# Block-sparse attention followed by a token and channel mixer: gates of pairs 1 to 5 by four column tiles, and a new order of late loads

## The chip, the cores and the metric

The kernel runs on one core of a Trainium2 chip. The metric is the time of one execution on the device in microseconds (us); less is better. The profile is that of one execution, and its times count from the start of its span.

## What is computed

The inputs are q, k and v of 4 batches, 8 heads, 768 positions and 64 channels, and four weight matrices. The part of the reference that matters here:

```
k_rep = k.reshape(B, H, n_blocks, block, D).mean(axis=3)        # 12 blocks of 64 keys
gate_scores = np.einsum('bhsd,bhnd->bhsn', q, k_rep)            # 768 queries x 12 blocks
gate_scores = np.where(causal, gate_scores, -1000000000.0)
top_idx = np.argsort(gate_scores, axis=-1)[..., -top_k:]        # top_k = 3, and the own block
...                                                             # a mask of the chosen blocks
scores = scale * np.matmul(q, k.transpose(0, 1, 3, 2))          # masked, causal, softmax
x = attention output, heads side by side (4, 768, 512)
h = np.maximum(xt @ w_tok1, 0.0) @ w_tok2                       # token mixing, 768 -> 256 -> 768
u = x + h.transpose(0, 2, 1)
h2 = np.maximum(u @ w_ch1, 0.0) @ w_ch2                         # channel mixing, 512 -> 1536 -> 512
return (u + h2).astype(np.float32)
```

The gate decides for each query which three blocks of keys it sees besides its own. It must be exact enough for the ranking, and so it is computed in 32-bit floats.

## The kernel before, in words

**Pairs.** Two heads of one batch make a pair; there are 16 pairs, four to a batch. Pair i goes through these steps, named as in the code (line numbers of the profile in brackets).

- Loads `kl` and `ql` (L315), two DMAs each on SyncE's queue, in the order kl.0, ql.0, kl.1, ql.1 and so on. A ring of three buffers holds each kind, so load i waits until the transposes of i-3 are done.
- Transposes `tr` of keys and queries on TensorE (L360), six 128x128 transposes each, and copies `kt` and `qt` out of PSUM by ScalarE (L369).
- Casts of kt and qt to 16 bits by GpSimd (L376), four of them for a pair. GpSimd also issues the loads of the values `v.i` (L322) and of the weights, which convert to 16 bits on the way. A load is put into GpSimd's program behind a cast that a table names: VAFTER for the values, WAIT for the weights.
- Block sums of the keys by VectorE (L389, L397), into `ks2`, 32 columns wide, of which 24 are used (two heads of 12 blocks).
- The gate. For pairs 0 to 5, `gate` (L407) holds 128 queries at a time as the stationary operand and streams the 24 columns of block sums: five such matmuls, for queries 128 to 767. Its result has queries on the partitions, which VectorE needs for the next step. Pairs 6 and 7, 8 to 11, and 12 to 15 go in groups: `gate_t` (L417) holds the block sums of each pair of the group in a 32-column tile of the array and streams the queries, so that the result is transposed; ScalarE copies it out (L427), and `gate_b` (L437) transposes it back.
- The ranking by VectorE (L449 or L453, L465, L473, L485), a transposition of the mask on TensorE (`mask`, L495), and two copies into rows 64 to 87 of the queries (L501), so that the scores matmul adds the mask by itself.
- For each head, scores in three parts (`sc`, L515), exponentials on ScalarE (L528), the causal corner on VectorE (L535), the product with the values (`av`, L547), and the division (L555, L566).

**Mixer.** When a batch has its four pairs, the token mixer (`tok1`, L578 or L609, and `umix`, L590 or L623) and the channel mixer follow: `ch1` (L659), 24 pieces of four matmuls, and `ch2` (L680), 18 pieces of four. They need the weights W0 and W1 (token), W2 to W5 (w_ch1 in quarters) and W6 to W9 (w_ch2 in quarters). Mixer work of one batch is put between the attention of the next.

**Order.** The program's order on every engine is written by `plan`, a list scheduler that runs when the program is built. Each step has an engine, a cost in ns, the steps it depends on, a priority, and buffers from rings. The costs and the sizes of transfers only decide the order; on the chip each engine runs its list in order and waits by semaphores. Where the planner sees TensorE free in the first 46 us it puts in small matmuls without use (`dummy`, L697), which keep the engine busy. PSUM holds two large tiles (`big`, for transposes, scores and the group gates) and three banks (`bank`, for the rest), so a transposition waits for a large tile whose copy by ScalarE is done.

The lines that decide the order of the loads:

```
O["v", i] = op("POOL", 1060, 0, last_av, vpre + 2, load_v(i), size=1350)
...
for i, (name, m) in enumerate(VAFTER):
    O["v", i].deps.append(O["cast", name, m, 1])
...
W.append(op("POOL", 700, 0, [O[("cast",) + WAIT[n]]], at, f, size=4500 if n < 2 else 2400 if n < 6 else 2800))
```

Of the kernel before, what the change touches and what calls it, by code (L numbers as in the profile page):

```python
# [9 lines left out]
FP = mybir.dt.float32  # L10
# [18 lines left out]
R = 5  # L29
# [10 lines left out]
def QACT(i):  # L40
    return i < 1


VAFTER = [("kt", 1), ("kt", 2), ("qt", 2), ("qt", 3), ("qt", 3), ("kt", 4), ("qt", 4), ("qt", 5),
          ("qt", 6), ("qt", 7), ("qt", 8), ("qt", 9), ("qt", 10), ("qt", 11), ("qt", 12), ("qt", 13)]
GATE = {2: 700, 3: 700, 4: 730}
GROUPED = [[0], [1], [2], [3], [4], [5], [6, 7], [8, 9, 10, 11], [12, 13, 14, 15]]
WAIT = [("kt", 3, 1), ("kt", 3, 1), ("qt", 3, 1), ("qt", 3, 1), ("qt", 4, 1), ("qt", 4, 1),
        ("qt", 5, 1), ("qt", 5, 1), ("qt", 6, 1), ("qt", 6, 1)]


class Op:
# [168 lines left out]
def kernel(  # L221
# [27 lines left out]

    pairs = [(b, h) for b in range(B) for h in range(0, H, 2)]  # L250
    NP = len(pairs)
    RINGS = dict(big=2, bank=3, av=1, ql=3, kl=3, qt=4, kt=2, gs=1, gt=1, gm=1, m8=1, bn=NBN, e0=3, e1=3, e2=3, rc=2,
                 x16=2, h1=2, u=2, uT=2, h2=1, ob=3)

    def sb(tag, shape, dt, name):
        return sp.tile(shape, dt, tag=tag, bufs=RINGS[tag], name=name)

# [25 lines left out]
    ident16 = sp.tile([128, 128], F16, tag="id16", name="id16")  # L283
    tri = sp.tile([128, 128], F16, tag="tri", name="tri")
    m0 = sp.tile([128, 128], F16, tag="m0", name="m0")
    warm = sp.tile([128, 256], F16, tag="warm", name="warm")
    spare = sp.tile([128, 8], F16, tag="spare", name="spare")

# [103 lines left out]
    def kcopy(i):  # L392
# [6 lines left out]
                                        axis=AX.X, op=ALU.add)  # L399
        return f  # L400

    def gate(i):
        def f():
            g = ps("bank", [128, GJ, 1, 2 * NB], "gps")
            T["gps", i] = g
            for j in range(GJ):
                nc.tensor.matmul(out=g[:, j, 0, :], lhsT=T["qt", i][:, 128 * j + 128:128 * j + 256],  # L407
                                 rhs=ks2[i % R][:, 0:2 * NB], start=True, stop=True)
        return f

    def gate_t(gi):
        def f():
            p = ps("big", None, "gtp")
            T["gtp", gi] = p
            for a, e in ((0, 512), (512, S - 128)):
                for s, i in enumerate(GROUPED[gi]):
                    nc.tensor.matmul(out=p[32 * s:32 * s + 32, a:e], lhsT=ks2[i % R],  # L417
                                     rhs=T["qt", i][:, 128 + a:128 + e], start=True, stop=True,
                                     tile_position=(0, 32 * s))
        return f  # L420

    def gate_e(gi):
        def f():
            n = 32 * len(GROUPED[gi])
            t = sb("gt", [128, S - 128], FP, f"gt_{gi}")
            T["gt", gi] = t
            nc.scalar.copy(out=t[0:n, :], in_=T["gtp", gi][0:n, 0:S - 128])  # L427
        return f

    def gate_b(gi):  # L430
        def f():
            n = 32 * len(GROUPED[gi])
            p = ps("big", None, "gbp")
            g = p[:, 0:128 * GJ].rearrange("p (j s c) -> p j s c", s=4, c=32)
            T["gps", GROUPED[gi][0]] = g[:, :, 0:len(GROUPED[gi]), 0:2 * NB]
            for j in range(GJ):
                nc.tensor.transpose(out=p[:, 128 * j:128 * j + n], in_=T["gt", gi][0:n, 128 * j:128 * j + 128],  # L437
                                    identity=ident32[0:n, 0:n])
        return f

# [275 lines left out]
    def prepare(i):  # L716
        b, h = pairs[i]
        gi = [n for n, G in enumerate(GROUPED) if i in G][0]
        i0 = GROUPED[gi][0]
        pre = 10.0 * (i0 - (AHEAD if i < FIRST else LATER)) + 2.5 * (i - i0) - (0 if len(GROUPED[gi]) == 1 else EXTRA)  # L720
        vpre = 10.0 * (i - (AHEAD if i < FIRST else LATER))
        old = i - R

        def last_scores(x):
            return [O.get(("sc", old, x, g)) for g in range(3)]

        for t32, src, off in (("kl", k, 0), ("ql", q, 0.1)):
            bf = Buf(t32)
            O[t32, i] = op("SP", 950, 0, [], pre - 12 + off, load_qk(i, t32, src), [bf], size=1750)
            big = Buf("big")  # L730
            O["tr", t32, i] = pe(660, [O[t32, i]], pre + off, transposes(t32, i), [big], tail=320)
            bf.users.append(O["tr", t32, i])
            name = "kt" if t32 == "kl" else "qt"
            tb = Buf(name)
            O[name, i] = act(768, [O["tr", t32, i]],
                             pre + 0.5 + off, evac_t(t32, i), [tb])
            big.users.append(O[name, i])
            dst = KA if name == "kt" else QA
            for x in range(2):
                occ = 770  # L740
                if QACT(i):
                    O["cast", name, i, x] = act(768, [O[name, i]] + last_scores(x), pre + 0.9 + 0.2 * x + off, cast_act(dst, name, i, x))
                    tb.users.append(O["cast", name, i, x])
                    continue
                O["cast", name, i, x] = op("POOL", occ, occ + 55, [O[name, i]] + last_scores(x), pre + 4 + off,
                                           cast(dst, name, i, x))
                tb.users.append(O["cast", name, i, x])
            if name == "kt":
                O["ksum", i] = dve(870, [O["kt", i]], pre + 1, ksum(i))
                tb.users.append(O["ksum", i])  # L750
                O["kcopy", i] = dve(200, [O["ksum", i], O.get(("gate", old))], pre + 1, kcopy(i))
            else:
                qb = tb
        last_av = [O.get(("av", i - R - 1, x)) for x in range(2)]
        O["v", i] = op("POOL", 1060, 0, last_av, vpre + 2, load_v(i), size=1350)
        n = len(GROUPED[gi])
        O["qb", i] = qb
        if i == GROUPED[gi][-1]:
            G = GROUPED[gi]
            if n == 1:  # L760
                gb = Buf("bank")
                O["gate", i] = gate_op = pe(1120, [O["kcopy", i], O["qt", i]], pre + 2, gate(i), [gb])
            else:
                tbig = Buf("big")
                gate_op = pe(GATE[n], [O["kcopy", m] for m in G] + [O["qt", m] for m in G], pre + 2, gate_t(gi), [tbig])
                for m in G:
                    O["gate", m] = gate_op
                gtb = Buf("gt")
                ge = act(S - 128, [gate_op], pre + 2.1, gate_e(gi), [gtb])
                tbig.users.append(ge)  # L770
                gb = Buf("big")
                gback = pe(550, [ge], pre + 2.2, gate_b(gi), [gb])
                gtb.users.append(gback)
            for m in G:
                O["qb", m].users.append(gate_op)
            gs = Buf("gs")
            O["gm", gi] = dve(75 + 125 * n, [gate_op] if n == 1 else [gback, own_op], pre + 3, gm(gi), [gs])
            gb.users.append(O["gm", gi])
            tops = [dve(720, [O["gm", gi]], pre + 3, top(gi, s)) if s == 0 else None for s in range(n)]
            for s in range(1, n):  # L780
                tops[s] = dve(720, [tops[0]], pre + 3, top(gi, s))
            O["lt", gi] = dve(75 + 125 * n, tops, pre + 3, below(gi))
            O["bias", gi] = dve((75 + 125 * n) if n == 4 else 200 * n, [O["lt", gi], O.get(("mask", gi - NBN))] + ([own_op] if n == 4 else []), pre + 3, bias(gi))
            gs.users += [O["bias", gi]]
            O["lt", gi].two = O["bias", gi].two = True
            mb = Buf("bank")
            O["mask", gi] = pe(280, [O["bias", gi]], pre + 4, mask(gi), [mb])
            for s, m in enumerate(G):
                for x in range(2):
                    O["put", m, x] = dve(410, [O["mask", gi]] + [O.get(("sc", m - R, x, g)) for g in range(3)],  # L790
                                         pre + 4, put_mask(gi, s, x))
                    mb.users.append(O["put", m, x])
# [45 lines left out]
        O["cast", "kt", 0, x].deps.append(O["qt", 0])  # L838
    O["ksum", 1].deps.append(O["bias", 0])
    for n, (at, f) in enumerate(wq):  # L840
        W.append(op("POOL", 700, 0, [O[("cast",) + WAIT[n]]], at, f, size=4500 if n < 2 else 2400 if n < 6 else 2800))

    for b in range(B):
        fill = 1000.0 * (b + 1)
# [78 lines left out]
    with tc.manual_schedule():  # L923
# [22 lines left out]
        nc.vector.memset(QAX[64:MK, :, :, 0:128], 0.0)  # L946
        for r in range(R + 1):
            nc.gpsimd.memset(V16[r][:, :, :, 64:65], 1.0)
        for y in range(NBN):
            nc.gpsimd.memset(bn16[y].bitcast(FP), 0.0)  # L950

# [35 lines left out]
```

## Time and profile before

| what | value |
|---|---|
| time, median of 5 runs | 264.81 us (263.87 to 266.32) |
| the profiled execution: its own time, its span | 264.81 us, 262.7 us |
| TensorE matmuls: busy, share of the span | 254.5 us, 97% |
| VectorE, ScalarE, GpSimd busy | 157.2, 145.3, 80.1 us |
| chain of work that ended last, TensorE's share | 92% |
| six direct gates (L407), matmuls | 60, start 8.4 to 48.8 us |
| three group gates (L417), matmuls | 40, start 60.6 to 136.1 us |
| V loads issued by GpSimd | 16, from 14.6 to 125.4 us |
| wc loads issued by GpSimd | 8, from 28.1 to 59.3 us |

A 32-bit matmul of the program is two instructions in the trace: five gate matmuls are ten. Matmuls overlap in the pipeline, so the cost of one is the distance from its start to the start of the next, not its duration. The view of waits says who waited for whom; the timeline of one engine shows in brackets how long it was idle before an instruction. A DMA lands when its last completion signal comes; these times are in the trace's DMA records.

### The profile page before, as it was taken

How to read it: one execution, taken by the hardware profiler on the slowest of the kernel's cores; microseconds unless marked ns; L12 is line 12 of the kernel's file. 1: busy time of each engine (PE TensorE's matmuls, PEld its weight loads, DVE VectorE, ACT ScalarE, POOL GpSimd, SP SyncE). 2: the span in 40 equal slices, each digit the busy share in tenths (PEclk: the TensorE clock that was granted, in tenths of full speed). 3: DMA queues.
4: the chain of work that ended last, by engine and by line, in shares of the span. 5: the costliest groups of instructions: out<-in, count | busy, mean ns of one | idle time of the engine just before them, and what ended most of it. 6: DMA issues, size and time to landing. Idle time of an engine off the chain costs nothing.

```text
span 262.7 us, 5828 instructions
## 1 busy us (share of the span) xinstructions
PE 254.5 (97%) x2296; PEld 165.9 (63%) x2296; DVE 157.2 (60%) x536; ACT 145.3 (55%) x195; POOL 80.1 (30%) x112
## 2 busy tenths in 40 slices
PE   8999999989899998999999999999999999999994
PEld 7988688875567685456656666654456544456443
DVE  3688769995967669985549965583243253333222
ACT  3877888857688964658863799940034400044000
POOL 8299638878236963245420000000000000000000
PEclk9999999999999999999999999999999999999999
DMA  8999999999999999187511000009220035300032
GB/s 167 221 187 192 204 189 190 189 190 190 184 135 214 191 209 125 40 115 117 72 41 44 0 2 0 2 0 202 80 80 2 0 63 137 130 32 0 2 146 93
DMA packets 91322, 28.77 MB, mean 110 GB/s; under 512 B 84896, under 2 KB 87840, under 8 KB 91296
## 3 DMA queue, kind: packets, MB, share of 16 engines
q1 hardware_dynamic: 63232, 21.33, 39.8%
q0 software_dynamic: 28064, 7.08, 27.2%
q8 instruction: 18, 0.29, 0.5%
q14 instruction: 8, 0.07, 0.1%
HBM read 26.83 MB, written 6.29 MB: 126 GB/s over the span
## 4 chain that ended last, share of the span: by engine, by line
PE 92%; DMA 3%; DVE 2%; ACT 1%; issue 1%; DVEq 0%; SPq 0%; ACTq 0%
PE c L659 24%; PE c L680 23%; PE sps L515 13%; PE avp L547 7%; PE tkl L360 4%; PE avp L697 3%; PE tql L360 3%; PE ups L590 3%; DMA kl<-in_k_dram 3%; PE gps L407 3%; PE tok L578 2%; PE gtp L417 1%; PE tok L609 1%; PE ups L623 1%; PE bps L495 1%
## 5 line engine op out<-in xcount | busy, mean ns | idle before, releaser
L528 ACT ACTIVATE e<-sps 128x1024 f16<-128x1024 f32 (+1 forms) x96 | 84.5, 920 | 15.8 <-PE sps L515 13.1
L659 PE MATMUL c<-uT,wc 128*128 128x256 f16 (+1 forms) x384 | 69.1, 326 | 0.0
L680 PE MATMUL c<-wc,h 128*128 128x512 f16 (+2 forms) x300 | 65.6, 370 | 0.0
L669 ACT ACTIVATE h<-c 128x512 f16<-128x512 f32 x48 | 28.7, 599 | 61.2 <-PE c L659 43.0
L659 PEld LDWEIGHTS <-wc 128*128 128x128 f16 x384 | 36.5, 98 | 23.0 <-issue 0.2
L515 PE MATMUL sps<-QA,KA 88*128 88x512 f16 (+3 forms) x256 | 50.2, 305 | 0.6 <-ACT e L528 0.6
L680 PEld LDWEIGHTS <-h 128*128 128x128 f16 x300 | 28.7, 98 | 30.5 <-issue 0.8
L376 POOL CAST KA<-kt 64x768 f16<-64x768 f32 x30 | 24.7, 824 | 44.3 <-ACT kt L369 27.0
L535 DVE TENSOR_TENSOR e<-e,m 128x256 f16<-128x256 f16 x90 | 28.1, 319 | 15.8 <-ACT e L528 15.1
L671 DVE TENSOR_SCALAR h<-c 128x256 f16<-128x256 f32 x48 | 20.3, 422 | 26.4 <-PE c L659 26.0
L688 DVE TENSOR_TENSOR ob<-u,c 128x512 f32<-128x512 f16 (+2 forms) x25 | 16.5, 664 | 32.2 <-PE c L680 32.1
L515 PEld LDWEIGHTS <-KA 88*128 88x128 f16 x256 | 22.9, 99 | 17.8 <-issue 1.2
L376 POOL CAST QA<-qt 64x768 f16<-64x768 f32 x30 | 25.7, 857 | 5.8 <-ACT qt L369 4.4
L547 PEld LDWEIGHTS <-e 128*128 128x128 f16 x672 | 25.3, 97 | 2.6
L547 PE MATMUL avp<-V,e 128*128 128x65 f16 x672 | 26.5, 193 | 0.0
L369 ACT COPY kt<-tkl 128x768 f32<-128x768 f32 x16 | 12.8, 799 | 11.7 <-PE tkl L360 8.4
L566 DVE TENSOR_TENSOR x<-avp,rc 128x384 f16<-128x384 f32 x32 | 17.8, 555 | 0.9
L389 DVE TENSOR_REDUCE kst<-kt 128x12 f32<-128x768 f32 x16 | 15.2, 950 | 5.0 <-ACT kt L369 4.6
L322 POOL DMA_DIRECT2D V<-in_v_dram x16 | 16.5, 1030 | 4.4 <-PE avp L547 3.2
L369 ACT COPY qt<-tql 128x768 f32<-128x768 f32 x16 | 12.8, 801 | 5.3 <-PE tql L360 5.1
L501 DVE COPY QA<-bps 24x640 f16<-24x640 f16 x32 | 14.3, 480 | 1.7 <-PE bps L495 1.4
L360 PE MATMUL tql<-id,ql 128*128 128x128 f32 x96 | 13.3, 275 | 1.9 <-ACT kt L369 1.0
(66 smaller groups left out, 212.8 us busy)
## 6 DMA issues: line engine op xcount, KB each, us to landing
kl<-in_k_dram SPq DMA_DIRECT2D x32, 192.0 KB, 5.8
ql<-in_q_dram SPq DMA_DIRECT2D x32, 192.0 KB, 5.9
out_dram<-ob SPq DMA_DIRECT2D x23, 256.0 KB, 2.0
V<-in_v_dram POOLq DMA_DIRECT2D x16, 192.0 KB, 7.1
wc<-in_moe_w_ch_dram POOLq DMA_DIRECT2D x8, 384.0 KB, 10.4
w<-in_moe_w_tok_dram POOLq DMA_DIRECT2D x2, 384.0 KB, 8.6
out_dram<-ob SPq DMA_DIRECT2D x1, 160.0 KB, 1.8
out_dram<-ob SPq DMA_DIRECT2D x1, 96.0 KB, 1.7
```

Source lines behind the costliest of these rows:

```text
L360: nc.tensor.transpose(out=p[:, 128 * j:128 * j + 128], in_=t[:, j, :], identity=ident32)
L369: nc.scalar.copy(out=t, in_=p[:, 0:S])
L376: nc.gpsimd.tensor_copy(out=to, in_=src)
L515: nc.tensor.matmul(out=p[:, off + a:off + a + n], lhsT=KA[i % R][x][0:MK, 128 * kk:128 * kk + 128], rhs=QA[i % R][x][0:MK, q0 + a:q0 + a + ...
L528: nc.scalar.activation(out=e[:, 0:width], in_=T["sps", i, x, g][:, 0:width], func=AF.Exp, scale=scale)
L535: nc.vector.tensor_tensor(out=d, in0=d, in1=m0.rearrange("p (a b) -> p a b", a=1).broadcast_to([128, 2, 128]), op=ALU.mult)
L547: nc.tensor.matmul(out=p[:, jq, :], lhsT=T["e", i, x, g][:, o:o + 128], rhs=V16[i % (R + 1)][:, x, kk, :], start=(kk == 0), stop=(kk == jq))
L566: nc.vector.tensor_tensor(out=T["x16", b][:, :, 64 * hh:64 * hh + 64], in0=T["aps", i, x][:, :, 0:64], in1=T["rc", i, x].broadcast_to([128 ...
L659: nc.tensor.matmul(out=p, lhsT=wc1_16[:, cc, 128 * fc:128 * fc + 128], rhs=T["uT", b][:, cc, a // 128:e // 128, :], start=(cc == 0), stop= ...
L669: nc.scalar.activation(out=T["h2", b][:, fc, a:e], in_=T["c1", b, fc, n], func=AF.Relu)
L671: nc.vector.tensor_scalar(out=T["h2", b][:, fc, a:e], in0=T["c1", b, fc, n], scalar1=0.0, scalar2=None, op0=ALU.max)
L680: nc.tensor.matmul(out=T["c2", b, j, lo], lhsT=T["h2", b][:, fc, 128 * j:128 * j + 128], rhs=wc2_16[:, fc, lo:hi], start=(fc == 0), stop=( ...
```

## The change

The gates of pairs 1 to 5 are computed as the groups are, but with one pair in all four column tiles: the same block sums are loaded into four 32-column tiles, and each tile streams another 128 of the pair's queries (queries 256 to 767). Four more matmuls of 64 columns cover queries 192 to 255 (all four tiles stream the same queries, so that all partitions of the result are written). Queries 128 to 191 can only choose among three blocks, all of which they see, and their gate values are set to zero once at the start. ScalarE copies 192 columns out (`gate_s`), and two transposes bring them back (`gate_r`): one of 32 partitions by 128 columns, one of 128 by 128. Pair 0 keeps the direct gate, now `gate_q`. The group gates leave out the same 64 queries: 576 columns in place of 640.

The tables VAFTER and WAIT name later casts: v.5 moves from behind the key cast of pair 4 to behind its query cast, v.6 to v.11 from behind the query casts of pairs 4, 5, 6, 7, 8, 9 to behind those of 6, 8, 11, 12, 13, 14, v.12 to the key cast and v.13 to v.15 to the query cast of pair 15. W6 and W7 move from the query cast of pair 5 to that of pair 6, W8 and W9 from that of 6 to that of 8. The planner's costs of gates and its sizes of V and of W6 to W9 change. The core of the diff:

```
-VAFTER = [("kt", 1), ("kt", 2), ("qt", 2), ("qt", 3), ("qt", 3), ("kt", 4), ("qt", 4), ("qt", 5),
-          ("qt", 6), ("qt", 7), ("qt", 8), ("qt", 9), ("qt", 10), ("qt", 11), ("qt", 12), ("qt", 13)]
-GATE = {2: 700, 3: 700, 4: 730}
+VAFTER = [("kt", 1), ("kt", 2), ("qt", 2), ("qt", 3), ("qt", 3), ("qt", 4), ("qt", 6), ("qt", 8),
+          ("qt", 11), ("qt", 12), ("qt", 13), ("qt", 14), ("kt", 15), ("qt", 15), ("qt", 15), ("qt", 15)]
+DIRECT = (0,)
+WSIZE = (2400, 4500)
+GATE = {1: 400, 2: 1000, 3: 1000, 4: 1000}
...
-        ("qt", 5, 1), ("qt", 5, 1), ("qt", 6, 1), ("qt", 6, 1)]
+        ("qt", 6, 1), ("qt", 6, 1), ("qt", 8, 1), ("qt", 8, 1)]
...
     def gate(i):
         def f():
-            g = ps("bank", [128, GJ, 1, 2 * NB], "gps")
-            T["gps", i] = g
-            for j in range(GJ):
-                nc.tensor.matmul(out=g[:, j, 0, :], lhsT=T["qt", i][:, 128 * j + 128:128 * j + 256],
-                                 rhs=ks2[i % R][:, 0:2 * NB], start=True, stop=True)
+            g = ps("bank", [128, 512], "gps")
+            T["gtp", i] = g
+            T["gps", i] = g[:, 192:192 + 32 * GJ].rearrange("p (j s c) -> p j s c", s=1, c=32)[:, :, :, 0:2 * NB]
+            for lo, at, n, step in ((256, 64, 128, 128), (192, 0, 64, 0)):
+                for s in range(4):
+                    nc.tensor.matmul(out=g[32 * s:32 * s + 32, at:at + n], lhsT=ks2[i % R],
+                                     rhs=T["qt", i][:, lo + step * s:lo + step * s + n], start=True, stop=True,
+                                     tile_position=(0, 32 * s))
+        return f
+
+    def gate_s(i):
+        return lambda: nc.scalar.copy(out=g1[i % 2][:, 64:256], in_=T["gtp", i][:, 0:192])
+
+    def gate_r(i):
+        def f():
+            g, t = T["gtp", i], g1[i % 2]
+            nc.tensor.transpose(out=g[:, 192:224], in_=t[0:32, 0:128], identity=ident32[0:32, 0:32])
+            nc.tensor.transpose(out=g[:, 224:352], in_=t[:, 128:256], identity=ident32)
         return f
...
-            for a, e in ((0, 512), (512, S - 128)):
+            for a, e in ((0, 512), (512, S - 192)):
...
-            nc.scalar.copy(out=t[0:n, :], in_=T["gtp", gi][0:n, 0:S - 128])
+            nc.scalar.copy(out=gt[0:n, 64:S - 128], in_=T["gtp", gi][0:n, 0:S - 192])
...
-        O["v", i] = op("POOL", 1060, 0, last_av, vpre + 2, load_v(i), size=1350)
+        O["v", i] = op("POOL", 1060, 0, last_av, vpre + 2, load_v(i), size=1800)
...
-                O["gate", i] = gate_op = pe(1120, [O["kcopy", i], O["qt", i]], pre + 2, gate(i), [gb])
+                split = i not in DIRECT
+                O["gate", i] = gback = gate_op = pe(GATE[1] if split else 1120, [O["kcopy", i], O["qt", i]], pre + 2, gate(i) if split else gate_q(i), [gb])
+                if split:
+                    tbuf = Buf("g1")
+                    gs1 = act(192, [gate_op], pre + 2.1, gate_s(i), [tbuf])
+                    gback = pe(190, [gs1], pre + 2.2, gate_r(i), tail=230)
+                    tbuf.users.append(gback)
+                    gb.users.append(gback)
...
-        W.append(op("POOL", 700, 0, [O[("cast",) + WAIT[n]]], at, f, size=4500 if n < 2 else 2400 if n < 6 else 2800))
+        W.append(op("POOL", 700, 0, [O[("cast",) + WAIT[n]]], at, f, size=WSIZE[n < 2]))
...
+        for t in g1 + [gt]:
+            nc.vector.memset(t[:, 0:64], 0.0)
```

More of the change, by code (lines that the diff above doesn't have):

```diff
@@ L251 @@
     NP = len(pairs)
-    RINGS = dict(big=2, bank=3, av=1, ql=3, kl=3, qt=4, kt=2, gs=1, gt=1, gm=1, m8=1, bn=NBN, e0=3, e1=3, e2=3, rc=2,
+    RINGS = dict(big=2, bank=3, av=1, ql=3, kl=3, qt=4, kt=2, gs=1, gt=1, g1=2, gm=1, m8=1, bn=NBN, e0=3, e1=3, e2=3, rc=2,
                  x16=2, h1=2, u=2, uT=2, h2=1, ob=3)
@@ L285 @@
     m0 = sp.tile([128, 128], F16, tag="m0", name="m0")
+    g1 = [sp.tile([128, 256], FP, tag=f"g1{y}", name=f"g1{y}") for y in range(2)]
+    gt = sp.tile([128, S - 128], FP, tag="gt", name="gt")
     warm = sp.tile([128, 256], F16, tag="warm", name="warm")
@@ L400, in kcopy, with gate_q, f @@
         return f
+    def gate_q(i):
+        def f():
+            g = ps("bank", [128, 512], "gps")
+            T["gps", i] = g[:, 0:2 * NB * GJ].rearrange("p (j s c) -> p j s c", s=1, c=2 * NB)
+            for j in range(GJ):
+                nc.tensor.matmul(out=T["gps", i][:, j, 0, :], lhsT=T["qt", i][:, 128 * j + 128:128 * j + 256],
+                                 rhs=ks2[i % R][:, 0:2 * NB], start=True, stop=True)
+        return f
     def gate(i):
         def f():
-            g = ps("bank", [128, GJ, 1, 2 * NB], "gps")
-            T["gps", i] = g
-            for j in range(GJ):
-                nc.tensor.matmul(out=g[:, j, 0, :], lhsT=T["qt", i][:, 128 * j + 128:128 * j + 256],
-                                 rhs=ks2[i % R][:, 0:2 * NB], start=True, stop=True)
+            g = ps("bank", [128, 512], "gps")
+            T["gtp", i] = g
[5 more added lines that the diff above has]
+                                     tile_position=(0, 32 * s))
+        return f
+    def gate_s(i):
+        return lambda: nc.scalar.copy(out=g1[i % 2][:, 64:256], in_=T["gtp", i][:, 0:192])
+    def gate_r(i):
+        def f():
+            g, t = T["gtp", i], g1[i % 2]
+            nc.tensor.transpose(out=g[:, 192:224], in_=t[0:32, 0:128], identity=ident32[0:32, 0:32])
+            nc.tensor.transpose(out=g[:, 224:352], in_=t[:, 128:256], identity=ident32)
         return f
@@ L414, in f @@
             T["gtp", gi] = p
-            for a, e in ((0, 512), (512, S - 128)):
+            for a, e in ((0, 512), (512, S - 192)):
                 for s, i in enumerate(GROUPED[gi]):
                     nc.tensor.matmul(out=p[32 * s:32 * s + 32, a:e], lhsT=ks2[i % R],
-                                     rhs=T["qt", i][:, 128 + a:128 + e], start=True, stop=True,
+                                     rhs=T["qt", i][:, 192 + a:192 + e], start=True, stop=True,
                                      tile_position=(0, 32 * s))
@@ L424, in f @@
             n = 32 * len(GROUPED[gi])
-            t = sb("gt", [128, S - 128], FP, f"gt_{gi}")
-            T["gt", gi] = t
-            nc.scalar.copy(out=t[0:n, :], in_=T["gtp", gi][0:n, 0:S - 128])
+            nc.scalar.copy(out=gt[0:n, 64:S - 128], in_=T["gtp", gi][0:n, 0:S - 192])
         return f
@@ L436, in f @@
             for j in range(GJ):
-                nc.tensor.transpose(out=p[:, 128 * j:128 * j + n], in_=T["gt", gi][0:n, 128 * j:128 * j + 128],
+                nc.tensor.transpose(out=p[:, 128 * j:128 * j + n], in_=gt[0:n, 128 * j:128 * j + 128],
                                     identity=ident32[0:n, 0:n])
@@ L768, in prepare @@
                 gtb = Buf("gt")
-                ge = act(S - 128, [gate_op], pre + 2.1, gate_e(gi), [gtb])
+                ge = act(S - 192, [gate_op], pre + 2.1, gate_e(gi), [gtb])
                 tbig.users.append(ge)
@@ L776, in prepare @@
             gs = Buf("gs")
-            O["gm", gi] = dve(75 + 125 * n, [gate_op] if n == 1 else [gback, own_op], pre + 3, gm(gi), [gs])
+            O["gm", gi] = dve(75 + 125 * n, [gback] if n == 1 else [gback, own_op], pre + 3, gm(gi), [gs])
             gb.users.append(O["gm", gi])
```

## The prediction

> **What bounds the kernel now.** I read the page first: the busy shares and the row of slices.
>
> ```profile
> PE 254.5 (97%) x2296; PEld 165.9 (63%) x2296; DVE 157.2 (60%) x536; ACT 145.3 (55%) x195; POOL 80.1 (30%) x112
> ...
> DMA  8999999999999999187511000009220035300032
> ```
>
> TensorE is busy nearly all the time, so the span is its work plus its few waits. But the DMA engines are full in the first 16 slices too (105 us), and after that nearly idle. So a second limit stands in the first 105 us: no key or query comes earlier than its transfer. The view of waits and TensorE's timeline show where the two meet.
>
> ```profile
> PE tkl L360 <- DMA kl<-in_k_dram: 1.0, 1, 1.0
> ...
> PE tql L360 <- issue: 0.9, 1, 0.9
> ```
>
> ```profile
> 57.63 0.85 PE L360 MATMUL tql<-id,ql 128*128 128x128 f32 x6 [0.86 <-issue]
> ...
> 70.28 0.85 PE L360 MATMUL tql<-id,ql 128*128 128x128 f32 x6 [1.01 <-ACT kt L369]
> ...
> 103.29 0.84 PE L360 MATMUL tkl<-id,kl 128*128 128x128 f32 x6 [0.98 <-DMA kl<-in_k_dram]
> ```
>
> The three long idle times of TensorE are all ahead of a transposition. The view names three causes, but the DMA records give one: ql.7 landed at 57.54, ql.8 at 70.15, kl.15 at 103.16 us, each 0.1 us before its transposes began. Measured from start to start, these cost 1.02, 1.17 and 1.14 us. After 15 us the other idle times are small: 0.24 at 24, 0.58 and 0.33 at 30 to 32 (exponentials), 0.20 at 175, and 0.48 at 210 to 212 (token mixer). 29 dummies stand in this stretch (1.6 us).
>
> **The gates on TensorE.**
>
> ```profile
> L407 PE MATMUL gps<-ks,qt 128*128 128x24 f32 x60 | 7.4, 265 | 0.1
> ...
> L417 PEld LDWEIGHTS gtp<-qt,ks 128*32 128x32 f32 x40 | 1.2, 109 | 2.7 <-issue 2.7
> ```
>
> The first row is the direct gate: ten instructions 112 ns apart, about 1.13 us for a pair. The second row is the form that the change spreads; its 2.7 us of idle belong to three gates. In the single instructions of the gate at 91.19 us, four tiles start 7 ns apart, a pass of four 128-column matmuls follows the one before by 109 ns, TensorE loses 0.09 us on the way into the 32-column form and 0.10 on the way out. The same 0.09 stands on both sides of the transposes of 64 partitions at 63.47 us (62 ns apart). A new gate is four passes: two of 128 columns (0.22 us) and two of 64, which no row has: between 62 ns, those transposes' pace, and 109, if the weight loads set the pace. With both switches 0.53 to 0.63; I take 0.57, nearer to the 62. The way back is a transposition in a form of its own (0.06, with 0.09 on either side) and a full one (0.11): 0.35, or 0.17 without the switches, 0.41 if the small one costs as the full one. So a pair costs 0.92 in place of 1.13: 0.2 us less, for five pairs **1.0 us** (0.45 to 1.25; if no switch cost anything, 2.9). The group gates lose 64 columns in two passes each: 0 to 0.3 us together.
>
> [...]
>
> **Beside it.** ScalarE gets five copies of 192 columns: from its 640 columns in 0.69 and 768 in 0.80, 0.32 us each, 1.6 in all. It is 55% busy, but from 24 to 34 us its exponentials follow each other without a break, and there the three copies of pairs 1 to 3 could cost up to 1.0. Against that, the exponentials at 18.10 waited 0.45 us for scores that stood behind the direct gate of pair 2, now shorter. A gate's result reaches VectorE about 0.4 us later (0.92 and 0.32 and two handovers, against 1.13), and VectorE is the link from 16 to 25 us; but the new order brings the key sums of pair 3 forward into that stretch. I take the early part as 0 to 1 us gained: the new order has 6 dummies fewer. Three small memsets go into VectorE's idle 3.2 us ahead of 6.9 us: nothing. If all this shortens the way to pair 7, what is late next is the load of keys and queries, and so it is priced there.
>
> **The loads, which decide.** In the new order TensorE takes the transposes of pair 6 some 8 us of work earlier, those of pair 7 by 2 to 3 us, and kl.8 by 12: it now stands directly ahead of the second `av` of pair 4, in place of behind the gate mask of pairs 6 and 7 (68.40 us). All that follows waits if kl.8 is late. Before, kl.8 landed at 63.51; TensorE gets to it by the row sums at about 55. So the question is how much earlier it lands.
>
> ```profile
> 47.35 1.71 POOL L376 CAST QA<-qt 64x768 f16<-64x768 f32 x2
> 49.00 1.51 POOL L713 DMA_DIRECT2D wc<-in_moe_w_ch_dram  x2
> 50.51 1.03 POOL L322 DMA_DIRECT2D V<-in_v_dram  x1
> ```
>
> GpSimd's queue is what steals from kl and ql. Counted in the packets of the DMA records, a wc load leaves the keys and queries 0.08 to 0.09 of a load per us, a V load 0.23 to 0.31, and alone they move 0.55. In full service a kl or ql takes 1.8 to 1.9 us, a V 1.5 to 1.9, a wc 1.9. GpSimd's program after the change is v.4, casts of pair 4, W4, W5, own_four, v.5, then the casts of pairs 5 and 6, and only then W6, W7, v.6. The casts of pair 5 began at 45.58; I put them at about 44.6, as TensorE is up to 1 us ahead. Four times 1.72 us of casts bring W6 to 51.5; from issue to its first packet such a load took 1.9 (58.56 to 60.47), so 53.4. Up to then the queue has V0 to V5 and W0 to W5 and nothing else, where before it also had all of v.6 and a quarter of W6. At 46 us 14.6 of the loads of keys and queries had gone. From there to 53.4 are 7.4 us of service; what is left of W4, W5 and V5 takes 2.9, and 4.5 are left, 2.4 loads: 16.9 to 17.0. kl.8 is the seventeenth. Its last tenth then runs beside W6 (1.1 us), and completion came 2.4 to 3.2 us after the last packet for loads beside wc (kl.7, ql.7, kl.8). So kl.8 lands at about **57.3**, and TensorE waits some 2 us there, once, where it waited 1.02 for ql.7. ql.7 itself lands by 53 to 54 and costs little.
>
> [...]
>
> Behind that point the DMA engines have less to carry: ql.8, kl.9 and the rest come 1.8 us apart, all ahead of their transposes, so the waits at 70.28 (1.17) and 103.29 (1.14; kl.15 is now transposed among `ch2` pieces, some 20 us later) go. W8, W9 and v.7 are issued at about 71 us; W9 is needed by the first `ch2` some 35 us later, v.7 by pair 7 at about 85, and a V took 4.6 to 16.3 to land: covered, but v.7 by least. v.8 to v.15 are wanted later still. The second token mixer now runs without scores between its pieces: 0.3 us more, as at 210 us.
>
> **The sum.** Call T the start of the transposes of kl.8. Before, the comparable point is the end of `av` of pair 4 at 56.62, with 198.6 us of work behind it (matmuls end at 259.4) and 4.2 of waits: 1.02, 1.17, 1.14 and 0.9 small ones. After, the work behind T is the same to 0.1 (ql.7's transposes done, one piece of 0.33 and the `av` still to do, group gates less 0.3), and waits of 1.2 (0.9 and 0.3). So the change of the time is T + 0.05 + 1.2 - 56.62 - 4.2, that is **T - 59.6**. The gates lie ahead of T, so their 1.0 us counts only if kl.8 is not late. With T = 57.3: -2.3. The profiled execution's own time is 264.81, equal to the median of the runs; its span is 262.7 and 2.1 lie outside it. Forecast **262.5 us**.
>
> **Rivals.** A difference of less than 0.5% (1.3 us) can't be told from no change here.
>
> - *All cover holds* (0.15): W6 comes a little later or the queue is empty a little earlier, kl.8 lands by 55, and TensorE doesn't wait: -4.6, 260.2 us. For it: 3 us of full service move 1.6 loads. Against it: ScalarE and the two large tiles must keep up with seven sets of transposes in 13 us.
> - *Given back* (0.20): T is near 59.3, one wait takes the place of three: -0.3, 264.5 us. A long landing (kl.8's 3.2 us behind its last packet) and an early W6 suffice.
> - *Slower, by kl.8 behind W6 and W7* (0.20): if the casts are done 1.5 us earlier, or W4, W5 and V5 run on past 53, kl.8 has 0.5 of a load to go when W6 and W7 start, gets 0.09 per us for 5 us, and lands at 61.3: +1.7, 266.5 us. It decides from T = 59.6.
> - The forecast itself (T from 55.8 to 58.3): 0.45.
>
> Faster by over 0.5% is the forecast and the first rival, 0.60; the second is within, 0.20; the third slower, 0.20. The range leaves out some of the first and the last: 260.0 to 266.5.
>
> **What would show it.** On TensorE's timeline an idle time ahead of the keys of pair 8 at 54 to 58 us and its end at the landing; no waits of over 0.5 us ahead of later transposes; L422 in passes of about 0.11 and 0.06 us with 0.09 on both sides; W6 issued at 51 to 52 us. I am wrong if kl.8 lands after 59.6, if a new wait stands on ScalarE's copies of pairs 5 to 8 or on v.7, or if the early part loses more than the loads gain.

## The result, and the profile after

The changed kernel takes 264.04 us, median of 53 runs (263.27 to 267.52); the kernel before took 264.72 in the same comparison (95 runs). The 267.52 is one run in a slower state, which the ratio leaves out; the next lower one is 265.00. The ratio is 0.9974, with a 95% interval of 0.9964 to 0.9984: a gain of 0.7 us (0.4 to 1.0), where 2.3 were forecast. The profiled execution took 264.19 us (before: 264.81), its span is 262.5 (262.7), and the last matmul starts at 258.83 (259.06). So 0.2 of the 0.6 us between these two executions lie in the span, and 0.4 outside it (2.1 us before, 1.7 after). That is no chance of one execution: wherever a run's span is on record, 2.0 to 2.15 us lie outside it for the kernel before and 1.66 to 1.77 for the changed one. So about half of the measured gain lies where the profile shows no work of an engine.

First the page of the changed kernel: busy shares, the slices of the DMA engines, and the chain of work that ended last.

```profile
PE 253.5 (97%) x2330; PEld 162.5 (62%) x2330; DVE 158.2 (60%) x539; ACT 146.4 (56%) x200; POOL 79.9 (30%) x112
...
DMA  8999999999999964493193000008220035300032
...
PE 72%; DVE 15%; DMA 6%; ACT 2%; issue 2%; POOL 1%; SPq 1%; DVEq 0%; ACTq 0%
```

The DMA engines are full for two slices less, as the loads were moved back. The third line is the news: the chain was 92% TensorE before, and now 15% of it is VectorE and 6% DMA. New waits stand on the path. The view of TensorE's waits names them:

```profile
PE avp L571 <- DVE e L559: 0.9, 1, 0.9
PE sps L539 <- ACT e L552: 0.8, 3, 0.4
PE c L683 <- DVE QA L525: 0.7, 2, 0.4
PE avp L571 <- DMA V<-in_v_dram: 0.6, 1, 0.6
PE bps L519 <- DVE bn L509: 0.6, 1, 0.6
```

None of the three waits of about 1 us ahead of a transposition is left. TensorE's timeline where the forecast put the one wait for kl.8:

```profile
54.48 0.82 PE L364 MATMUL tkl<-id,kl 128*128 128x128 f32 x6
55.15 0.82 PE L364 MATMUL tql<-id,ql 128*128 128x128 f32 x6
...
56.63 0.83 PE L364 MATMUL tkl<-id,kl 128*128 128x128 f32 x6
57.29 0.82 PE L571 MATMUL avp<-V,e 128*128 128x65 f16 x21
```

These are kl.7, ql.7 and kl.8, and no bracket stands behind them. In the DMA records kl.8 landed at 55.62, a whole us ahead of its transposes. So T, on which the forecast hung, is 56.63 (forecast 57.3): by its sum the change should be -3.0. It was lost behind that point:

```profile
85.15 0.82 PE L571 MATMUL avp<-V,e 128*128 128x65 f16 x21 [0.61 <-DMA V<-in_v_dram]
...
103.06 0.60 PE L683 MATMUL c<-uT,wc 128*128 128x256 f16 x4 [0.30 <-DVE QA L525]
...
106.76 0.68 PE L571 MATMUL avp<-V,e 128*128 128x65 f16 x16 [0.94 <-DVE e L559]
...
141.68 0.60 PE L683 MATMUL c<-uT,wc 128*128 128x256 f16 x4 [0.41 <-DVE QA L525]
```

The brackets count idle time; from start to start, less the usual pace, the four cost 0.77, 0.46, 1.10 and 0.58 us, 2.9 together. The first is v.7, issued behind W8 and W9 at 72.53 and landed at 85.11. The other three are VectorE: a mask copy that frees a bank (L525) in two of them, a causal corner (L559) in the longest. The view of the chain runs through it from 91.08 to 106.71 without a break. The last part of that on VectorE's timeline:

```profile
97.57 1.80 DVE L393 TENSOR_REDUCE kst<-kt 128x12 f32<-128x768 f32 x2
99.40 3.60 DVE L525 COPY QA<-bps 24x640 f16<-24x640 f16 x8
103.03 0.39 DVE L559 TENSOR_TENSOR e<-e,m 128x256 f16<-128x256 f16 x1
103.35 0.67 DVE L401 TENSOR_REDUCE ks<-kst 64x12 f32<-64x12 f32 x4
104.05 0.69 DVE L622 TENSOR_TENSOR u<-x,ups 128x512 f16<-128x512 f16 x1
104.65 0.42 DVE L695 TENSOR_SCALAR h<-c 128x256 f16<-128x256 f32 x1
104.98 0.28 DVE L559 TENSOR_TENSOR e<-e,m 128x256 f16<-128x256 f16 x1
105.18 0.68 DVE L622 TENSOR_TENSOR u<-x,ups 128x512 f16<-128x512 f16 x1
105.78 0.92 DVE L559 TENSOR_TENSOR e<-e,m 128x256 f16<-128x256 f16 x1
```

The values of the group gate of pairs 8 to 11 come back at 90.34; from there VectorE ranks four pairs, copies eight masks (3.6 us) and owes the first `av` of pair 8 three corners (L559), with key sums of the next group and mixer additions queued between them. The last corner starts at 105.78. TensorE's timeline from the same gate's return to the first `av` of pair 8, before and then after:

```profile
94.00 0.71 PE L437 MATMUL gbp<-id,gt 128*128 128x128 f32 x5
...
113.37 0.83 PE L547 MATMUL avp<-V,e 128*128 128x65 f16 x21
```

```profile
90.34 0.71 PE L461 MATMUL gbp<-id,gt 128*128 128x128 f32 x5
...
105.50 0.32 PE L571 MATMUL avp<-V,e 128*128 128x65 f16 x5
```

Before, the stretch took 19.4 us, for TensorE still had `ch2` and six `umix` pieces to do, and that `av` didn't wait. After, TensorE asks for pair 8 some 15.2 us behind the gate, and VectorE's last corner is done after 16.4; the `av` stops behind five of its 21 matmuls.

### The profile page after: what moved, and what is told of

It reads as the page before. It is cut to its first block, busy times and chain, and to the rows that moved or that the text cites. A ratio compares the mean times of both kernels' runs of the same rounds, so it can differ in the third digit from the quotient of the medians.

```text
span 262.5 us, 5901 instructions
## 1 busy us (share of the span) xinstructions
PE 253.5 (97%) x2330; PEld 162.5 (62%) x2330; DVE 158.2 (60%) x539; ACT 146.4 (56%) x200; POOL 79.9 (30%) x112
## 4 chain that ended last, share of the span: by engine, by line
PE 72%; DVE 15%; DMA 6%; ACT 2%; issue 2%; POOL 1%; SPq 1%; DVEq 0%; ACTq 0%
PE c L704 21%; PE c L683 20%; PE sps L539 10%; PE avp L571 6%; DMA V<-in_v_dram 5%; DVE QA L525 3%; DVE m L489 3%; PE ups L614 3%; PE tql L364 2%; PE tok L602 2%; PE tkl L364 2%; DMA ql<-in_q_dram 1%; ACT e L552 1%; PE gtp L443 1%; DVE e L559 1%
## 5 line engine op out<-in xcount | busy, mean ns | idle before, releaser
L683 PE MATMUL c<-uT,wc 128*128 128x256 f16 (+1 forms) x384 | 69.9, 326 | 0.9 <-DVE QA L525 0.7
L704 PE MATMUL c<-wc,h 128*128 128x512 f16 (+2 forms) x300 | 64.8, 370 | 0.0
L539 PE MATMUL sps<-QA,KA 88*128 88x512 f16 (+3 forms) x256 | 50.8, 306 | 0.9 <-ACT e L552 0.8
L559 DVE TENSOR_TENSOR e<-e,m 128x256 f16<-128x256 f16 x90 | 29.1, 333 | 13.1 <-ACT e L552 12.5
L525 DVE COPY QA<-bps 24x640 f16<-24x640 f16 x32 | 14.3, 480 | 1.1 <-PE bps L519 0.8
L622 DVE TENSOR_TENSOR u<-x,ups 128x512 f16<-128x512 f16 x18 | 11.6, 681 | 3.9 <-PE ups L614 3.8
```

Of the source, the lines that this page charges most:

```text
L525: nc.vector.tensor_copy(out=QA[i % R][x][64:MK, 128:S], in_=T["bps", gi][32 * s:32 * s + 2 * NB, :])
L539: nc.tensor.matmul(out=p[:, off + a:off + a + n], lhsT=KA[i % R][x][0:MK, 128 * kk:128 * kk + 128], rhs=QA[i % R][x][0:MK, q0 + a:q0 + a + ...
L559: nc.vector.tensor_tensor(out=d, in0=d, in1=m0.rearrange("p (a b) -> p a b", a=1).broadcast_to([128, 2, 128]), op=ALU.mult)
L683: nc.tensor.matmul(out=p, lhsT=wc1_16[:, cc, 128 * fc:128 * fc + 128], rhs=T["uT", b][:, cc, a // 128:e // 128, :], start=(cc == 0), stop= ...
L704: nc.tensor.matmul(out=T["c2", b, j, lo], lhsT=T["h2", b][:, fc, 128 * j:128 * j + 128], rhs=wc2_16[:, fc, lo:hi], start=(fc == 0), stop=( ...
```

## Experiments

All times are medians; each ratio is to the kernel before, run beside it, with its 95% interval. "Behind" in a diff puts a step directly behind another in the finished order of its engine and changes nothing else. In the diffs `ksum` and `kcopy` are the two steps of a pair's block sums on VectorE, `put` is a mask copy, and `uadd` a mixer addition. The granted clock is the share of its full clock that TensorE was given, as the profile shows it.

A profile is one execution, and executions differ: the first transposes, at 5 us, took 0.85 us in the profile of the changed kernel, 1.31 in that of the kernel before, 1.50 in 3 and 1.52 in 12, and the first gate starts anywhere from 8.1 to 9.1 us. What makes them longer was not shown. Where it matters, it is said.

**1. The new gates with the old loads**, planned anew.

```
VAFTER and WAIT, and the planner's sizes of V (1350) and of W6 to W9 (2800), as before
```

> The changed kernel with the old places and sizes of the value and weight loads; only the gates are new, and the planner orders anew. Theory (the gates lie ahead of a point that the key and query loads set, so their 0.13 us each are lost there): within 0.5 us of before, about 264.6 us, and the waits ahead of the transposes of ql.7, ql.8 and kl.15 stay, some 3 us together. Rival (TensorE's work is the bound everywhere): 0.7 to 1.3 us less than before, about 263.7.

275.81 us (1.0410, 1.0365 to 1.0455). Both missed by 11 us or more. I had not foreseen that the planner, with the old tables and sizes, would put the transposes of kl.7, kl.8 and ql.8 well ahead of their loads:

```profile
51.27 0.85 PE L364 MATMUL tkl<-id,kl 128*128 128x128 f32 x6 [2.15 <-DMA kl<-in_k_dram]
...
64.28 1.51 PE L364 MATMUL tkl<-id,kl 128*128 128x128 f32 x6 [3.54 <-DMA kl<-in_k_dram]
69.51 1.51 PE L364 MATMUL tql<-id,ql 128*128 128x128 f32 x6 [3.72 <-DMA ql<-in_q_dram]
```

The last two rows take 1.51 us instead of 0.82, at a granted clock of 0.50 (the mean from 64.3 to 65.4 us, and from 69.4 to 72.0): behind these waits the clock was lower, too (below). What it shows is an order that its loads can't follow; it doesn't price the gates.

**2. The loads with direct gates**, planned anew.

```
-DIRECT = (0,)
+DIRECT = (0, 1, 2, 3, 4, 5)
```

> The changed kernel with the direct gate for all of pairs 0 to 5; the new loads and the narrower group gates stay, and the planner orders anew. Theory (the loads bring the gain, the gates nothing): the same as the changed kernel within 0.5 us, about 264.0, with no wait for keys of over 0.5 us. Rival (the gates bring the gain and the loads nothing): as before, about 264.7, with waits ahead of the transposes of pairs 7 and 8.

262.88 us (0.9918, 0.9885 to 0.9951): 2.2 us faster than before and 1.2 (by the medians) to 1.5 (by the ratios) faster than the changed kernel. The last matmul starts at 256.94. Waits for v.7, for the mask's bank and for the corners are absent; behind 96 us nothing waits over 0.25. Theory and rival both missed: neither had the direct gates faster than the changed kernel.

**3. v.7 ahead of W8** in the changed kernel.

```
+    order.remove(O["v", 7])
+    order.insert(order.index(W[8]), O["v", 7])
```

> The changed kernel with one step moved in GpSimd's program, all other orders as they were: v.7 is issued ahead of W8 and W9. Theory (the late landing of v.7 at 85.11 us costs its whole wait, since the ranking of the next group hangs on what follows): the wait of 0.77 us ahead of the first product with the values of pair 7 goes, 0.6 to 0.8 us less than the changed kernel, about 263.3. Rival (VectorE sets the pace between 90 and 107 us anyway, and the wait is hidden): 0 to 0.2 less, and the waits at 102 to 107 us grow by what was won.

263.57 us (0.9957, 0.9929 to 0.9985). v.7 lands at 77.58 and its wait is gone, but the interval holds the changed kernel's 0.9974 too, and in the profile TensorE is no sooner at the end (last matmul 258.78): that execution lost 0.7 us in its first transposes, before 9 us. The waits at 102 to 107 us stand as they were (0.45 and 1.10), so what was won did not move there, as the rival had it. A gain of about 0.5 us by the ratios, between theory and rival and not established. One reason shows in experiment 9, where v.7 was not moved: in that execution it landed at 84.33, and nothing waited for it. So the 0.77 is what the wait cost in the profiled execution, and not in each.

**4. W6, W7 and v.6 as early as before** in the changed kernel.

```
+    behind(W[6], O["cast", "qt", 5, 1]); behind(W[7], W[6]); behind(O["v", 6], W[7])
```

> The changed kernel with W6, W7 and v.6 issued behind the query casts of pair 5, 3.4 us earlier, as before the change; all other orders as they were. Theory (loads on GpSimd's queue keep kl.8 away, and TensorE's order hangs on kl.8): kl.8 lands near 61 us in place of 55.6, TensorE waits some 4 us ahead of its transposes, and the time is 3.5 to 4.5 us over the changed kernel, about 268. Rival (keys and queries have slack, what counts is the order alone): within 0.5 us of the changed kernel.

269.73 us (1.0167, 1.0122 to 1.0212), 4.4 over before. kl.8 lands at 60.68, 5.1 later, and TensorE waits 3.33 for it (T = 60.81), as the rival "slower, by kl.8 behind W6 and W7" had it. The time is 5.1 us over the changed kernel by the ratios, more than the theory's 3.5 to 4.5. A large part of the rest is the clock, 0.50 behind that wait. The windows (time, PE, PEld, DVE, ACT, POOL busy, granted clock, DMA share, GB/s):

```profile
57.40:60.80 3.40, 0.25 (x5) 0.09 (x3) 3.15 (x5) 0.35 (x1) 3.00 (x4) 0.83 1.48 171
60.80:64.00 3.20, 3.19 (x30) 2.80 (x31) 0.39 (x3) 0.80 (x1) 0.73 (x1) 0.50 1.29 201
64.00:67.00 3.00, 3.00 (x16) 1.52 (x14) 1.39 (x4) 2.05 (x2) 0.91 (x2) 0.59 1.09 226
67.00:70.00 3.00, 3.00 (x22) 1.45 (x22) 2.01 (x6) 1.95 (x4) 0.00 (x0) 1.00 1.14 217
```

The clock is 0.50 from 60.8 to 64.0 us, 0.59 on average to 67.0, and 1.00 behind that. With the 0.59 as a mix of 0.50 and 1.00, half the clock ends at about 66.5 us, and over these 5.7 us it costs up to 2.8 us, an estimate from the windows.

**5. The loads alone in the order of before.**

```
+    W6, W7, v.6 behind cast.qt.6; v.7 behind cast.qt.8; W8, W9 behind cast.kt.9
+    v.8 to v.11 behind cast.qt.11 to cast.qt.14
```

> The kernel before, all orders as they were, except GpSimd's: W6, W7 and v.6 behind the casts of pair 6, v.7 behind those of pair 8, W8 and W9 behind the first of pair 9, v.8 to v.11 behind those of pairs 11 to 14. Theory (the loads bring the gain, whatever the gates are): ql.7, ql.8 and kl.15 land ahead of their transposes, the waits of 1.02, 1.17 and 1.14 at 57.6, 70.3 and 103.3 us shrink below 0.3 each, and 262.0 to 262.8 us. Rival (the gain needs the new order that the planner makes of the new sizes and gates; here the same waits only move to W, V or ScalarE): 264.2 to 265.2.

265.57 us (1.0018, 0.9992 to 1.0045). The waits for ql.7 and ql.8 are gone: the transposes of kl.9 start at 76.59 instead of 78.97. But v.8, now at 90.3, came together with v.12 and v.13, which I had left at 91.4 and 93.3, and kl.15, issued at 93.7, landed at 102.26:

```profile
99.70:102.40 2.70, 0.23 (x5) 0.09 (x3) 2.64 (x6) 0.99 (x2) 0.00 (x0) 1.00 1.58 208
102.40:105.40 3.00, 3.00 (x12) 1.59 (x13) 1.59 (x4) 0.00 (x0) 0.00 (x0) 0.61 0.80 60
105.40:108.40 3.00, 3.00 (x15) 1.39 (x13) 1.41 (x4) 1.86 (x3) 0.00 (x0) 0.82 0.00 0
```

A wait of 2.63 us, and 1.7 us more by the clock, an estimate from its 0.61 and 0.82 in the two windows behind the wait. What was won was given back 25 us later, and the time is over the rival's range.

**6. The same with v.12 to v.15 moved too**, as in the changed kernel.

```
+    v.12 behind cast.kt.15; v.13 to v.15 behind cast.qt.15
```

> As the kernel before with GpSimd's loads moved, and v.12 moved too, behind the first casts of pair 15, v.13 to v.15 behind the last. In the run before this the gain was 2.38 us by the transposes of kl.9 (76.59 for 78.97 us) and then lost at kl.15, which waited 2.63 us behind v.8, v.12 and v.13, issued at 90.3 to 93.3 us, with 1.4 us more at half the clock after it. Theory (the loads alone, well placed, bring some 2 us in the old order too): kl.15 lands ahead of its transposes, 261.6 to 262.8 us. Rival (something else stands behind kl.15, so the gain is lost all the same): 264.2 to 265.2.

263.05 us (0.9928, 0.9899 to 0.9956), -1.9 us. The median lies between theory and rival, 0.25 over the theory's range. The loads alone bring the gain, with no new order. The profiled execution is the slowest of its seven (264.12); in it ql.14 still makes TensorE wait 1.9 us at 97.8, so v.8, issued at 90.7, probably still comes too early.

**7. The new gates in the order of before**, loads as before: copy directly behind the gate, way back ahead of VectorE's first step.

```
+    order.insert(index(gate.i) + 1, gate_s(i)); order.insert(index(gm.i), gate_r(i))    # i = 1 to 5
```

> The kernel before, all orders as they were, with the gates of pairs 1 to 5 in the four 32-column tiles: the copy directly behind the gate in ScalarE's order, the way back directly ahead of the gate mask's first VectorE step. Theory (the form itself costs nothing; it saves some 0.13 us of TensorE a pair, but all five pairs lie ahead of the wait for ql.7 at 57.6 us, which takes the gain up): no change, 264.3 to 265.0 us. Rival (the form costs what lies between the changed kernel and the same with direct gates, 1.1 us, through the copies on ScalarE and the later bias): 265.5 to 266.5.

268.89 us (1.0158, 1.0127 to 1.0190), slower than the rival too. TensorE's timeline:

```profile
18.42 0.38 PE L539 MATMUL sps<-QA,KA 88*128 88x512 f16 x1 [0.87 <-ACT e L552]
...
19.99 0.24 PE L421 MATMUL gps<-id,g 32*128 32x32 f32 x1
...
24.54 0.45 PE L519 MATMUL bps<-id,bn 128*32 128x128 f16 x5 [1.78 <-DVE bn L509]
```

The way back of pair 2 stands 3.5 us behind its gate at 16.52, and pair 2's mask waits 1.9 us for VectorE. By the transposes of kl.6 4.6 us are lost (56.93 for 52.29); the waits for loads that vanish behind it give 2.2 back (last matmul 261.49; the profiled execution, 267.81, is the fastest of its six). The edit's place of the way back is part of that, so it is the price of form and place together, and not of the form alone.

**8. Both in the order of before** (5 and 7 together).

> The two edits before this together: the kernel before with the new gates and GpSimd's loads moved, and all else in the order that it had. Theory (what the changed kernel lost, it lost to its new order behind 57 us): as the loads alone or up to 0.6 better, 261.5 to 262.6 us. Rival (the gates' form costs 1.1 us wherever it stands): 263.2 to 264.2, the time of the changed kernel.

270.07 us (1.0212, 1.0181 to 1.0243). It has the loss of 7, the wait at kl.15 of 5 (1.7 us), and 3.4 us at half clock between 26 and 30, an estimate from its means of 0.55 (26 to 28) and 0.60 (28 to 30). Neither the theory nor the rival held, and it tells no more than 5 and 7.

**9. VectorE's order around 98 to 106 us** in the changed kernel.

```
+    behind(ksum.13, put.11.1); the 2nd and 3rd corner of pair 8 behind their exponentials
+    behind(kcopy.12, uadd.1.2); behind(kcopy.13, kcopy.12)
```

> The changed kernel, only VectorE's order changed around 98 to 106 us: the key sums of pair 13 behind the last mask copy of pairs 8 to 11, the two diagonals of pair 8 directly behind their exponentials, the copies of the key sums of pairs 12 and 13 behind the third mixer addition. Theory (TensorE's waits of 0.46 at 102.4 and 1.10 at 105.6 us are VectorE's order, and nothing takes their place): 262.5 to 263.2 us. Rival (ScalarE's exponentials or the mixer's banks are late next, so the waits move by a few us): 263.8 to 264.4.

263.04 us (0.9941, 0.9918 to 0.9964), inside the theory's range and 0.9 us under the changed kernel by the ratios; the two intervals only touch. TensorE's timeline:

```profile
103.17 0.60 PE L539 MATMUL sps<-QA,KA 88*128 88x512 f16 x3
104.29 0.59 PE L614 MATMUL ups<-h,w 128*128 128x512 f16 x2 [0.53 <-DVE u L622]
104.72 0.44 PE L539 MATMUL sps<-QA,KA 88*128 88x512 f16 x2
105.00 0.83 PE L571 MATMUL avp<-V,e 128*128 128x65 f16 x21
```

The `av` follows without a wait; of 1.56 us 0.69 come back at the first `umix` pieces, where a mixer addition is late next.

**10. 9 and 3 together.**

> The changed kernel with VectorE's order around 98 to 106 us changed as before and v.7 ahead of W8 in GpSimd's order. Theory (the forecast missed by the waits behind the transposes of kl.8, and they are independent): 0.9 and 0.5 us add up, 262.3 to 262.9 us, and so about the time forecast for the changed kernel. Rival (v.7's 0.77 us only lets TensorE come earlier to the next wait, as its single profile suggested): 263.0 to 263.3.

263.07 us (0.9928, 0.9906 to 0.9951), -1.9 us. By its median the rival, by its ratio the theory; against 9 (0.9941) the difference is inside the intervals.

**11. Two edits more:** the key sums of pair 13 behind `uadd.1.2`, and `ch1.1.0.1` behind `sc.12.1.0`.

> As the run before it, and two edits more in the changed kernel: the key sums of pair 13 behind the third mixer addition too (for the 0.5 to 0.7 us that the first umix pieces still wait at 103.4), and on TensorE the second ch1 piece of the second token batch behind the fourth scores of pair 12 (for the 0.6 us at 139.4 to 141 in which it waits for a bank that the mask copies hold). Theory (all waits behind kl.8 that the forecast left out are gone): 261.3 to 262.3 us. Rival (each moves on to ScalarE or the next bank): 262.4 to 263.0.

263.01 us (0.9924, 0.9898 to 0.9950), as the rival had it. The wait at 103 to 104 is gone; the one at 140 only changed its owner:

```profile
140.38 0.61 PE L539 MATMUL sps<-QA,KA 88*128 88x512 f16 x3 [0.46 <-ACT e L552]
```

**12. Direct gates in the changed kernel's own order:** ten direct instructions where the four tiles stood, copies and ways back left out, nothing else moved.

> The changed kernel in its own order, loads and all, with only the form of the gates of pairs 1 to 5 undone: ten direct instructions where the four tiles stood, and the copies and the ways back left out. Theory (in this order the new form saves TensorE 0.13 us a pair, 0.65 in all, and nothing takes it up, as kl.8 lands 1.0 us ahead of its transposes): 264.4 to 264.9 us. Rival (the form costs more through VectorE's later bias, 0.75 us at 23.2, and ScalarE's five copies, 1.6 us in all, than it saves): 263.0 to 263.7 us.

265.66 us (1.0026, 1.0001 to 1.0050): 1.4 us slower than the changed kernel, over the theory's range and far from the rival. In its profile the transposes of kl.8 start at 58.41 for 56.63; 0.5 of that is there at 7 us, ahead of any new gate (its first transposes took 1.52 us). v.7's wait is absent, as TensorE comes later; the 1.10 at 106 us and the 0.58 at 142 stand as before. So in this order the form brings 1.3 us in the traces, 1.4 by the ratios (some 0.7 to 2.1, an estimate from the two intervals).

Kernels 2, 6, 10 and 11 beat both kernels of the change, all by about 2 us against before; their intervals do not part them.

## Why the forecast was wrong

**The step that failed** is in the sum: "and waits of 1.2 (0.9 and 0.3)" behind T. Measured are 4.2: small ones of the size that was put in (0.30 at 59.6 us, 0.47 at 174, 0.48 at 211, together 1.25) and the 2.9 that were not foreseen. With T = 56.63 the formula gives -3.0, and with the 2.9 it gives -0.1; the last matmul moved by -0.23. Another 0.4 us lie outside the span, which I had taken as fixed. Kernels 5 and 6, which change the order of loads alone, have 2.0 to 2.1 us outside it; all the others have the 1.7 of the changed kernel, also with direct gates (2, 12). What makes the difference was not tried. I looked for waits on loads, as that was what the waits of before were, and not at what TensorE would ask of VectorE once it came 3.7 us sooner (90.34 for 94.00 at the return of the group gate). Experiments 9 to 11 show it: only orders on VectorE, one load and one TensorE piece are changed, and the gain grows from 0.7 to between 1.6 and 2.0 us.

- **The gates' price** was right, that of the way back 0.08 too low. The single instructions have passes at 14.93, 15.06, 15.17 and 15.23 and the next work at 15.40, 0.57 us with both switches as forecast; the way back takes 0.43 (0.35). So a pair saves 0.13 us of TensorE, not 0.2, and five save 0.65. Yet in its own order the form is worth 1.3 us (12), near the 1.0 forecast: the other half is spread over small waits that stand elsewhere with direct gates (2.8 us instead of 2.5 between 19 and 35 us, 0.29 at 45 and 55) and was not taken apart further.
- **"0 to 1 us gained" in the early part** came out as 0: the transposes of kl.4 start at 35.35 (35.39). Pair 2's mask waits 0.75 for VectorE at 23.1, and waits for exponentials follow. (The kernel before did have a break in its exponentials between 24 and 34 us, 0.76 at 29.64, which I had overlooked; it didn't decide anything.)
- **W6 at 51.5, kl.8 at 57.3**: 52.51 and 55.62. W6 was a us late, and the landing was mild: kl.8 came 1.6 us after the seventeenth load's last packet (54.0), not 2.4 to 3.2. That T came within 0.7 us was luck: the forecast had TensorE there at about 55.3 and then a wait of 2 us for kl.8. In the run kl.8 was there first, and T is when TensorE's own work was done, 1.3 us later than forecast; that fits an early part that gained nothing. "All cover holds" had the right cause, with a landing by 55 and -4.6: TensorE didn't wait for kl.8, but it came there at 56.63, and the rest of the gain was lost behind it.
- **The loads decide**: right (2 and 6, about 2 us each, with direct gates; in 2, 0.4 of it lies outside the span). That kl.8 behind W6 and W7 makes it slower, too (4), though the 4.4 us are more than the formula's 1.2 for T = 60.8: the clock (0.50 and 0.59 in the windows of 4) and the later waits were not in it.
- **The waits at 70.28 and 103.29 go**: right. "v.7 by least" was named and priced at nothing, and a wait on v.7 was among the signs of being wrong: in the profiled execution it cost 0.77.
- **Beyond the steps:** with the same tables of loads, direct gates in the order planned for them (2) are 2.9 us faster by the ratios than the same gates in the order planned for the new ones (12). The costs given for a few gates at 15 to 50 us made the planner write another order up to 140 us; of the difference in the two traces (2.9 us as well) the three VectorE waits of 12 are 2.1, and 0.6 are there at the first gate (8.82 for 8.22 us). Why the planner's order is better for one set of costs than for the other was not tried.

## What to carry to other kernels

When a change lets the bounding engine run ahead, write down for each later stage how long the other engines need from its input to its output (here 16 us of VectorE from the group gate to the first `av`) and compare it with the work that the bounding engine still has to put there; do this for every stage up to the end, not only for the stage in which the old waits stood. A table of costs that steers a scheduler is itself an edit of the whole program: price parts of such a change with the finished order held fixed, as in 6, 9 and 12. A moved load has to be checked against the loads that stay (5).

## What the runs showed of the hardware

The granted clock was 0.50 behind some of TensorE's long waits, and which of them bring that on was not shown. The stretches at half clock below are estimates from the windows' mean clocks, each taken as a mix of 0.50 and 1.00, the lowest and the highest that a window has.

- In 5 it was 1.00 in the wait of 2.63 us itself (99.7 to 102.4), then 0.61 to 105.4 and 0.82 to 108.4: 3.4 us at half clock, which cost another 1.7 us.
- In 4, with a wait of 3.33 us, it was 0.83 from 57.4 to 60.8, most of which is the wait, 0.50 to 64.0 and 0.59 to 67.0: 6.8 us.
- In 1, with two waits of about 3.7 and 4.0 us and 1.2 us of work between them, it was 0.94 from 60.5 to 64.3, 0.50 from there to 74.0 and 0.99 to 77.0: 10.2 us.
- In 7 and 8 TensorE was idle for 1.78 us of the stretch from 22 to 26 us, in 7 all of it ahead of the mask at 24.54 us (1.94 from start to start). In 8 the clock was then 0.55 from 26 to 28 and 0.60 to 30, together 3.4 us at half clock; in 7 it was 1.00 up to 32.
- No half clock followed the wait of 1.9 us in 6 (1.000 over the whole execution), nor that of 2.4 us at 51.27 us in 1 (the six transposes behind it take 0.85 us, and the clock is 1.00 from 57.0 to 60.5).
